# The sign of a 64-bit weight made by ScalarE's scaling, and the list scheduler's settings beside it

## The chip, the cores and the metric

One core of a Trainium2 chip runs the whole program in one launch. The metric is the device time of that launch in microseconds (us), the median of the runs shown. Engines: TensorE (PE, its weight loads PEld), VectorE (DVE), ScalarE (ACT), GpSimd (POOL) and SyncE (SP), which issues every DMA here.

## What is computed

Attention for 4 batches of 8 heads (576 tokens, head size 64), with every score more than tau below its row's maximum masked out, then two feed-forward networks over the 2304 tokens:

```python
scores = scale * np.matmul(q, k.transpose(0, 1, 3, 2))
thresh = np.max(scores, axis=-1, keepdims=True) - tau
scores = np.where(scores >= thresh, scores, -1000000000.0)
attn = softmax(scores)                       # written out in the reference
x = matmul(attn, v), heads side by side      # 2304 x 512
h = (x @ w1) * (x @ w2) @ w3
x = h @ w_out                                # 1024 -> 512
h = x @ w_in                                 # 512 -> 2048
out = (h * sigmoid(h)) @ w_out2              # 2048 -> 512
```

The weights arrive as 64-bit floats, all else as 32-bit.

## The kernel before

Nothing is in source order: each call describes one operation to a planner (`Plan.op`, with engine, estimated time, buffers read and written), and `Plan.run` then writes out a list schedule. It always takes the operation that can start first; a priority (`plan.base`) decides only among those that compete for an engine at that moment. `merge` gives the priorities: it interleaves a list of attention steps with a list of matrix-product steps by their cost and moves the attention steps forward by a lead (`LEAD` for the first merge, `LEADS[i]` for the next four).

The five merges are: attention of batch 0 beside the product w34 of w3 and w_out (`w34_step`, line 1181); then four times the layers of one token group (`moe_steps`, products on line 1131) beside the attention of the next batch, the last one alone. A group is 576, 432, 432 and 864 tokens, in tiles of 288 or 432.

A head pair's attention (`qtiles`): scores on line 759 into one of two PSUM slots, the row maximum by VectorE on line 726, then for each tile one of two ways to mask. Either ScalarE masks by a parametric ReLU (line 791) and exponentiates (line 799), or ScalarE exponentiates (line 809) and VectorE masks (line 817). `MASK_DVE` gives, for each batch, the share of the second way. For batches after 0 the result stays in the PSUM slot; for batch 0 it goes to SBUF tile e (`STAY`). Then high and low half of p (lines 858 and 865), transposes by DMA, and the product with v (line 935).

Precision is kept by splitting every 32-bit operand into a high part (ScalarE copy) and a low part (a subtraction, `pool_sub`, GpSimd on line 472, or VectorE on line 466 for every n-th one as `ON_DVE` says, keyed by kind and merge). Kind "w lo" splits weights, "split lo" splits activations.

The 64-bit weights are turned into 32-bit ones on the core, once: `load32` loads a tile in two DMAs, `words` converts it, and for group 0 the result is stored (line 1060) for the later groups to load. 36 tiles of 1 MB are converted, 12 of them (w3, w_out) in the first merge and 24 in the second. The conversion of one tile is a chain of four: ScalarE multiplies the high word, read as a 32-bit float, by 2 to the power -112 (line 1083); VectorE shifts the bits left by 3 (line 1090), puts the sign bit of the high word in (line 1097), and puts in the top of the low word (line 1105).

Of the kernel before, what the change touches and what calls it, by code (L numbers as in the profile page):

```python
# [7 lines left out]
F32 = mybir.dt.float32  # L8
F32R = mybir.dt.float32r
# [29 lines left out]
PSCALE = 2.0 ** 15  # L39
VSCALE = 2.0 ** 14  # L40

LEAD = 40.0
LEADS = 0.0, 40.0, 20.0, 0.0

EVERY = 100, 100

ON_DVE = {("w lo", 1): 3}

MASK_DVE = 0.4, 0.2, 0.6, 0.8

STAY = False, True, True, True
EARLY_OUT = False
KH_POOL = False

PORT = {"p lo", "w shift", "w sign", "w low", "w lo", "vl", "kl", "ql", "v scale"}
class Buf:


# [266 lines left out]
def fused_kernel(  # L325
# [21 lines left out]
    def pool(name, n, shape, dt):  # L347
        p = ctx.enter_context(tc.tile_pool(name=name, bufs=1))
        plan.cap(name, n)
        return buf(name, lambda slot: p.tile(shape, dt, tag=f"{name}{slot}", name=f"{name}{slot}"))  # L350

    def fixed(name, shape, dt):
        b = Buf()
        b.tile = const.tile(shape, dt, name=name)
        return b
# [21 lines left out]
    qk_b = pool("qk", 1, [128, 2, S], F32)  # L377
    vr_b = pool("vr", 1, [128, 2, 9, D], F32)
    vs_b = pool("vs", 2, [128, 16], F32)
    kh_b = pool("kh", 2, [128, S], F32R)  # L380
    kl_b = pool("kl", 2, [128, S], F32R)
    e_b = pool("e", 2, [128, S], F32)
    hl_b = pool("hl", 3, [128, 2 * S], F16)
    st_b = pool("st", 4, [128, 12], F32)
# [49 lines left out]
        return t.rearrange("p (a n) -> p a n", a=2)  # L434

    def mm(n, width, f32r=False):
        return n * max(width * 0.4167 + 2.5, 133.4 if f32r else 0.0) + 3

    def dma(kind, move, fn, r=(), w=(), hold=(), turn=False):
        plan.op(kind, "SP", plan.TURN_ISSUE if turn else plan.ISSUE, fn, r, w, hold, move, turn)  # L440
# [37 lines left out]
    sc = fixed("sc", [128, 1], F32)  # L478
    tau8 = fixed("tau8", [128, 1], F32)
    eb = fixed("eb", [128, 1], F32)  # L480
    qs = [[fixed(f"qs{j}{i}", [128, 640], F32R) for i in range(2)] for j in range(2)]
    vst = [fixed(f"vst{j}", [128, 14, 128], F16) for j in range(2)]
    ones = fixed("ones", [128, 128], F32)
    w34 = dram_p.tile([4, 128, 8, 128], F32, name="w34")
# [4 lines left out]
    def setup():  # L489
        dma("tau load", 56, lambda: nc.sync.dma_start(out=tau_sb.t, in_=tau), w=[tau_sb])  # L490

        def consts():


            nc.vector.tensor_scalar(
                out=tau8.t, in0=tau_sb.t, scalar1=0.0, scalar2=1.0, op0=ALU.is_ge, op1=ALU.subtract
            )
            nc.vector.tensor_scalar(
                out=sc.t, in0=tau8.t, scalar1=1.0, scalar2=0.125, op0=ALU.add, op1=ALU.mult
            )  # L500
            nc.vector.tensor_scalar(
                out=tau8.t, in0=tau8.t, scalar1=3.0e38, scalar2=None, op0=ALU.mult
            )
            nc.vector.scalar_tensor_tensor(
                out=tau8.t, in0=tau_sb.t, scalar=-8.0, in1=tau8.t, op0=ALU.mult, op1=ALU.min
            )
            nc.vector.tensor_tensor(out=eb.t, in0=sc.t, in1=tau8.t, op=ALU.mult)

        def zeros():
            for i in range(2):  # L510
                nc.vector.memset(qs[0][i].t[:, 576:640].bitcast(F32), 0.0)
                nc.vector.memset(qs[1][i].t[:, 0:64].bitcast(F32), 0.0)
            nc.vector.memset(ones.t, 1.0)

        plan.op("zeros", "DVE", 437, zeros, w=[*qs[0], *qs[1], ones])
        for j in range(2):
            plan.op(
                "v zeros", "POOL", 780,
                lambda j=j: nc.gpsimd.memset(vst[j].t[:, :, 64 - 64 * j:128 - 64 * j], 0.0),
                w=[vst[j]],  # L520
            )
        plan.op("consts", "DVE", 840, consts, r=[tau_sb], w=[sc, tau8, eb])
# [2 lines left out]
    raws, kst = {}, {}  # L525

    def load_qk(g):
        qk = qk_b()
        came = [Buf(), Buf()]
        if g:  # L530
            dma("qk load", 1638, lambda: nc.sync.dma_start(out=qk.t, in_=qkv[g, :, 0:2, :]), w=[qk])
            came = [qk, qk]
        else:
            for n in range(2):
                dma(
                    "qk load", 819,
                    lambda n=n: nc.sync.dma_start(out=qk.t[:, n], in_=qkv[g, :, n, :]),
                    w=[came[n]], hold=[qk],
                )
        raws[g] = (qk, came)  # L540

    def prep_qk(g):

        j, i = g % 2, (g // 2) % 2
        r, (cq, ck) = raws.pop(g)
        o = 0 if j == 0 else 64
        q = qs[j][i]
        kh, kl = kh_b(), kl_b()

        def sub(kind, out, a, b, need, w):  # L550
            if g:
                pool_sub(kind, S, out, a, b, need, w, [r])
            else:
                plan.op(
                    kind, "DVE", 676,
                    lambda: nc.vector.tensor_tensor(out=out(), in0=a(), in1=b(), op=ALU.subtract),
                    need, w, [r],
                )

        def copy(kind, out, a, need, w):  # L560
            if KH_POOL and 0 < g < 2 * NP:
                plan.op(kind, "POOL", 900, lambda: nc.gpsimd.tensor_copy(out=out(), in_=a()), need, w, [r])
            else:
                act_op(kind, S, lambda: nc.scalar.activation(out=out(), in_=a(), func=ACTF.Copy), need, w, [r])  # L564

        copy("qh", lambda: q.t[:, o:o + S], lambda: r.t[:, 0, :], [cq], [q])
        sub(
            "ql", lambda: q.t[64:128, o:o + S], lambda: r.t[64:128, 0, :],
            lambda: q.t[64:128, o:o + S].bitcast(F32), [cq, q], [q],
        )  # L570
        copy("kh", lambda: kh.t, lambda: r.t[:, 1, :], [ck], [kh])
        sub("kl", lambda: kl.t, lambda: r.t[:, 1, :], lambda: kh.t.bitcast(F32), [ck, kh], [kl])
        kst[g] = (kh, kl)

# [108 lines left out]
    def qtiles(pr, kinds):  # L683
# [3 lines left out]

        ga, gb = 2 * pr, 2 * pr + 1
        i = pr % 2
        qa, qb = qs[0][i], qs[1][i]  # L690
        n_t = len(kinds)
        st = st_b()
        k_s = [Buf() for _ in kinds]
# [60 lines left out]
            plan.base += 1e4  # L754

        def scores(sp, mms):
            for n, (q, o, k) in enumerate(mms):
                for a in range(2):
                    nc.tensor.matmul(  # L759
                        out=sp.t[:, a, 0:HALF], lhsT=q.t[:, o:o + 128],  # L760
                        rhs=k.t[:, a * HALF:(a + 1) * HALF],
                        start=(n == 0), stop=(n == len(mms) - 1),
                    )

        sps = []
        for n, (kind, c) in enumerate(kinds):
            if kind == "A":
                terms = [(qa, c * 128, kst[ga])]
            elif kind == "B":
                terms = [(qb, 128 + c * 128, kst[gb])]  # L770
            else:
                terms = [(qa, 512, kst[ga]), (qb, 0, kst[gb])]
            mms = [(q, o, k) for q, o, ks in terms for k in ks]
            sp = s_b()
            plan.op(
                "scores", "PE", len(mms) * mm(2, HALF, True), lambda sp=sp, mms=mms: scores(sp, mms),
                [q for q, _, _ in mms] + [k for _, _, k in mms], [sp],
            )
            sps.append(sp)
            thresholds(sp, n)  # L780
# [251 lines left out]
    def load32(src, key=None, keep=None, rs=None):  # L1032

        if src.dtype == F32:
            r = wr_b()  # L1040
            dma("w load", 1456, lambda: nc.sync.dma_start(out=r.t, in_=src), key, [r])
            return r
        r = rs[0] if rs else wr_b()
        d = r64_b()
        came = [Buf(), Buf()]
        for a in range(2):
            cut = slice(a * 512, (a + 1) * 512)
            dma(
                "w64 load", 1456,
                lambda cut=cut: nc.sync.dma_start(  # L1050
                    out=d.t[:, cut],
                    in_=src[:, cut].bitcast(I32).rearrange("p (n t) -> p n t", t=2),
                ),
                w=[came[a]], hold=[d],
            )
        n = 1024 // len(rs or [r])
        for i, r in enumerate(rs or [r]):
            words(d, r, came, i * n, n)
        if keep is not None:
            dma("w keep", 1456, lambda: nc.sync.dma_start(out=keep, in_=r.t), [r], key)  # L1060
        return r
# [4 lines left out]
    def words(d, r, came, c0, n):  # L1066
# [11 lines left out]
        def rf():  # L1078
            return f32(r.t)[:, 0:n]
# [1 line left out]
        act_op(  # L1081
            "w scale", n,
            lambda: nc.scalar.activation(
                out=rf(), in_=high().bitcast(F32), func=ACTF.Copy, scale=2.0 ** -112
            ),
            came, [r], hold=[d],
        )
# [3 lines left out]
                out=ri(), in0=ri(), scalar1=3, scalar2=None, op0=ALU.logical_shift_left  # L1091
            ),
            [r], [r],
        )
        plan.op(
            "w sign", "DVE", 73 + n * 1.042,
            lambda: nc.vector.scalar_tensor_tensor(
                out=ri(), in0=high(), scalar=-0x80000000, in1=ri(),
                op0=ALU.bitwise_and, op1=ALU.bitwise_or,
            ),  # L1100
            [r], [r], hold=[d],
        )
        plan.op(
            "w low", "DVE", 73 + n * 1.042,
# [396 lines left out]
```

## Time and profile before

| | us |
|---|---|
| median of 3 runs | 1023.28 |
| lowest, highest | 1021.57, 1027.87 |
| the profiled execution, time | 1024.79 |
| its span from first to last instruction | 1023.0 |
| busy in the span: PE, PEld | 960.1, 863.6 |
| busy in the span: DVE, ACT, POOL | 605.0, 684.6, 509.8 |

Some words on reading it. The span is one execution; busy time is what an engine spent in instructions that compute. Matmuls are pipelined and their ends are modelled, so that a PE that reads as busy need not run at its peak. An idle time before an instruction is put down to the releaser that came last. PEclk is the clock that TensorE was granted, as a share of the full one. The DMA share is the mean busy share of 16 DMA engines. In the views by line, a group shows the engine, the operation, what it writes and reads, the shapes, the count, then busy us and mean ns of one.

### The profile page before, as it was taken

To read this page: it belongs to the slowest core of one execution; us is meant where nothing else is said; L and a number is where in the kernel's file an instruction comes from. 1 tells how busy PE (TensorE), PEld (TensorE's weight loads), DVE (VectorE), ACT (ScalarE), POOL (GpSimd) and SP (SyncE) were. 2 spreads that over 40 slices of the span, in tenths; PEclk is the share of its full clock that TensorE was granted. 3 is DMA by queue.
4 is the path that set the end of the run, shared out by engine and by line. 5 is a ranking of instruction groups with operands and counts; after the bars stand their busy time and mean duration, and the time that the engine had idled before them with its cause. 6 is when DMAs were issued, how large, how long until landed. Compare 5 with 4: busy or idle time off the path is not lost.

```text
span 1023.0 us, 15583 instructions
## 1 busy us (share of the span) xinstructions
PE 960.1 (94%) x5488; PEld 863.6 (84%) x5488; DVE 605.0 (59%) x1238; ACT 684.6 (67%) x1225; POOL 509.8 (50%) x306
## 2 busy tenths in 40 slices
PE   3579998999899996999999999999999999999998
PEld 3455658999899886999999999889989999999998
DVE  6988988777888886667666766666721111210211
ACT  7868967887888977788988787788733322432430
POOL 2221132653564543576859666675744542652650
PEclk9879999999999998999999999999999999999999
DMA  7999999987799987677778886776641111111111
GB/s 227 210 241 232 264 259 284 266 231 209 195 255 271 244 224 198 153 183 190 186 193 186 210 204 184 161 181 153 154 127 62 62 50 54 62 62 42 62 59 53
DMA packets 213934, 175.09 MB, mean 171 GB/s; under 512 B 175328, under 2 KB 181472, under 8 KB 213856
## 3 DMA queue, kind: packets, MB, share of 16 engines
q1 hardware_dynamic: 213856, 174.10, 66.5%
q8 instruction: 43, 0.70, 0.3%
q14 instruction: 35, 0.29, 0.1%
HBM read 112.20 MB, written 19.40 MB: 129 GB/s over the span
## 4 chain that ended last, share of the span: by engine, by line
PE 68%; DMA 11%; DVE 8%; ACT 7%; issue 4%; POOL 2%; SPq 1%; ACTq 0%; DVEq 0%; POOLq 0%
PE banks L1131 55%; PE banks L759 6%; PE banks L935 5%; DMA qk<-qkv 3%; PE banks L1181 2%; DMA r<-w3t 2%; DVE hl L865 2%; DMA pt<-hl 1%; DMA r<-w 1%; DMA r<-win 1%; DVE banks L726 1%; DMA wr<-w 1%; ACT hl L858 1%; POOL lo L472 1%; ACT hi L453 1%
## 5 line engine op out<-in xcount | busy, mean ns | idle before, releaser
L1131 PE MATMUL banks<-acts,hi 128*128 128x432 f32 (+1 forms) x1664 | 417.7, 337 | 5.9 <-DVE tb L1317 4.9
L472 POOL TENSOR_TENSOR lo<-wr,hi 128x1024 fp32r<-128x1024 f32 x102 | 247.9, 2431 | 221.0 <-PE banks L1131 101.9
L1131 PEld LDWEIGHTS banks<-acts,hi 128*128 128x128 f32 x1664 | 290.8, 188 | 16.7 <-DVE tb L1317 6.9
L1131 PE MATMUL banks<-acts,lo 128*128 128x432 f32 (+1 forms) x832 | 278.0, 334 | 0.3 <-POOL lo L472 0.3
L1131 PE MATMUL banks<-x,hi 128*128 128x432 f32 (+1 forms) x1024 | 267.4, 345 | 2.2 <-POOL x L472 1.0
L472 POOL TENSOR_TENSOR acts<-tb,acts 128x432 fp32r<-128x432 f32 (+1 forms) x120 | 150.8, 1262 | 85.5 <-ACT acts L1218 84.9
L1131 PEld LDWEIGHTS banks<-x,hi 128*128 128x128 f32 x1024 | 184.2, 189 | 10.3 <-POOL x L472 1.3
L1131 PE MATMUL banks<-x,lo 128*128 128x432 f32 (+1 forms) x512 | 176.3, 344 | 0.1
L1131 PEld LDWEIGHTS banks<-acts,lo 128*128 128x128 f32 x832 | 156.2, 188 | 5.1 <-POOL lo L472 0.6
L453 ACT ACTIVATE hi<-wr 128x1024 fp32r<-128x1024 f32 x112 | 118.3, 1057 | 28.0 <-DMA wr<-w 15.2
L726 DVE TENSOR_REDUCE banks<-banks 128x1 f32<-128x576 f32 x144 | 106.8, 758 | 29.1 <-PE banks L759 28.6
L759 PE MATMUL banks<-kh,qs 128*128 128x288 f32 x320 | 82.0, 340 | 43.5 <-ACT e L799 16.4
L1317 DVE SCALAR_TENSOR_TENSOR tb<-ta,banks 128x432 f32<-128x432 f32 (+1 forms) x96 | 52.8, 550 | 108.0 <-ACT ta L1310 103.3
L935 PE MATMUL banks<-pt,vst 128*128 128x288 f16 x656 | 102.5, 297 | 5.9 <-DMA pt<-hl 5.6
L759 PEld LDWEIGHTS banks<-kh,qs 128*128 128x128 f32 x320 | 57.2, 204 | 57.7 <-ACT e L799 20.6
L472 POOL TENSOR_TENSOR qs<-qk,qs 64x576 fp32r<-64x576 f32 x31 | 49.1, 1585 | 111.5 <-ACT qs L564 89.2
L865 DVE SCALAR_TENSOR_TENSOR hl<-banks,st,hl 128x576 f16<-128x576 f32 x108 | 84.1, 812 | 31.3 <-ACT hl L858 30.7
L1131 PEld LDWEIGHTS banks<-x,lo 128*128 128x128 f32 x512 | 96.3, 188 | 3.4 <-POOL lo L472 0.3
L935 PEld LDWEIGHTS <-vst 128*128 128x128 f16 x656 | 60.1, 101 | 40.9 <-issue 20.2
L1218 ACT ACTIVATE acts<-tb 128x432 fp32r<-128x432 f32 (+1 forms) x120 | 70.5, 587 | 34.3 <-DVE tb L1317 22.3
L858 ACT ACTIVATE hl<-banks,st 128x576 f16<-128x576 f32 x108 | 75.1, 737 | 8.8 <-DVE st L831 8.6
L759 PE MATMUL banks<-kl,qs 128*128 128x288 f32 x320 | 73.3, 312 | 0.0
(82 smaller groups left out, 1126.7 us busy)
## 6 DMA issues: line engine op xcount, KB each, us to landing
wr<-w SPq DMA_DIRECT2D x88, 512.0 KB, 3.6
qk<-qkv SPq DMA_DIRECT2D x31, 576.0 KB, 4.8
r<-wo SPq DMA_DIRECT2D x24, 512.0 KB, 6.0
w<-wr SPq DMA_DIRECT2D x24, 512.0 KB, 3.5
vr<-qkv SPq DMA_DIRECT2D x16, 576.0 KB, 4.7
r<-w3t SPq DMA_DIRECT2D x16, 512.0 KB, 5.6
r<-w SPq DMA_DIRECT2D x16, 512.0 KB, 6.1
r<-win SPq DMA_DIRECT2D x16, 512.0 KB, 5.9
```

Source lines behind the costliest of these rows:

```text
L453: kind, n, lambda: nc.scalar.activation(out=out(), in_=a(), func=ACTF.Copy), r, w, hold, ns
L472: lambda: nc.gpsimd.tensor_tensor(out=out(), in0=a(), in1=b(), op=ALU.subtract),
L726: lambda: nc.vector.tensor_reduce(out=low(), in_=sp.t[:, :, 0:HALF], axis=AX.XY, op=ALU.max, negate=True),
L759: nc.tensor.matmul(out=sp.t[:, a, 0:HALF], lhsT=q.t[:, o:o + 128], rhs=k.t[:, a * HALF:(a + 1) * HALF], start=(n == 0), stop=(n == len(mms ...
L858: lambda: nc.scalar.activation(out=two(hl.t[:, 0:S]), in_=src(), func=ACTF.Copy, scale=r()),
L865: lambda: nc.vector.scalar_tensor_tensor(out=two(hl.t[:, S:2 * S]), in0=src(), scalar=r(), in1=two(hl.t[:, 0:S]), op0=ALU.mult, op1=ALU.su ...
L935: nc.tensor.matmul(out=ps[a].t[:, 0:HALF], lhsT=v2.t[:, n, :], rhs=pt.t[:, c, a * HALF:(a + 1) * HALF], start=(first and n == 0), stop=(fi ...
L1131: nc.tensor.matmul(out=ps.t[:, 0:n1 - n0], lhsT=a_.t[:, k * 128:(k + 1) * 128], rhs=x_.t[:, n0:n1], start=(n == 0 and i == 0), stop=(n == ...
L1181: lambda jb=jb, x=x: nc.tensor.matmul(out=ps.t[:, 0:512], lhsT=f32(r.t)[:, jb * 128:(jb + 1) * 128], rhs=x.t[:, 0:512].bitcast(F32), start ...
L1218: lambda: nc.scalar.activation(out=hi.t[:, at[0]:at[1]], in_=x32.t[:, 0:n], func=ACTF.Copy),
L1317: lambda ps=ps, t=t, n=n, o=o, g32=g32: nc.vector.scalar_tensor_tensor(out=g32.t[:, o:o + n], in0=t.t[:, 0:n], scalar=1.0, in1=ps.t[:, 0:n ...
```

## The change

ScalarE's scaling of the high word becomes a parametric ReLU with slope -(2 to the power 32) for negative inputs. For a negative weight the product is then positive with an exponent field larger by 32, and the shift left by 3 moves the bit of value 32 of that field into the sign's place. The VectorE operation for the sign, line 1097, is dropped.

With it settings change: the leads, the share of masks on VectorE, the subtractions on VectorE, and `EARLY_OUT`, by which batch 0's mask on ScalarE writes to SBUF tile e instead of back to the PSUM slot. The planner's price of a matmul of 32-bit floats is 0.4517 ns a column and 2.9 ns instead of 0.4167 and 2.5 with a floor of 133.4. Query and key of head 0 come by one DMA instead of two, and the four query tiles get their zeros a second time before their first use. The diff also holds a path for whole heads (`WHOLE`), which is 0, so that nothing of it is issued; buffers for q and k are named in another pool with the same sizes.

```diff
-LEAD = 40.0
-LEADS = 0.0, 40.0, 20.0, 0.0
+LEAD = 100
+LEADS = 20, 20, 40, 0

-ON_DVE = {("w lo", 1): 3}
-MASK_DVE = 0.4, 0.2, 0.6, 0.8
+ON_DVE = {("w lo", 1): 2, ("split lo", 1): 2}
+MASK_DVE = 0.5, 0.2, 0.6, 0.6

-EARLY_OUT = False
-KH_POOL = False
+EARLY_OUT = True
+WHOLE = 0
...
     def mm(n, width, f32r=False):
-        return n * max(width * 0.4167 + 2.5, 133.4 if f32r else 0.0) + 3
+        return n * (width * 0.4517 + 2.9 if f32r else width * 0.4167 + 2.5) + 3
...
-        came = [Buf(), Buf()]
-        if g:
-            dma("qk load", 1638, lambda: nc.sync.dma_start(out=qk.t, in_=qkv[g, :, 0:2, :]), w=[qk])
-            came = [qk, qk]
-        else:
-            for n in range(2):
-                dma(
-                    "qk load", 819,
-                    lambda n=n: nc.sync.dma_start(out=qk.t[:, n], in_=qkv[g, :, n, :]),
-                    w=[came[n]], hold=[qk],
-                )
-        raws[g] = (qk, came)
+        dma("qk load", 1638, lambda: nc.sync.dma_start(out=qk.t, in_=qkv[g, :, 0:2, :]), w=[qk])
+        raws[g] = (qk, [qk, qk])
...
+        if H * WHOLE <= g < H * WHOLE + 4:
+            plan.op("q zeros", "DVE", 70, lambda: q_zeros(j, i, False), w=[q])
...
             lambda: nc.scalar.activation(
-                out=rf(), in_=high().bitcast(F32), func=ACTF.Copy, scale=2.0 ** -112
+                out=rf(), in_=high().bitcast(F32), func=ACTF.Prelu, scale=2.0 ** -112,
+                alpha=-(2.0 ** 32),
             ),
...
-        plan.op(
-            "w sign", "DVE", 73 + n * 1.042,
-            lambda: nc.vector.scalar_tensor_tensor(
-                out=ri(), in0=high(), scalar=-0x80000000, in1=ri(),
-                op0=ALU.bitwise_and, op1=ALU.bitwise_or,
-            ),
-            [r], [r], hold=[d],
-        )
```

## Rows read from the trace of the kernel before

**Rows 1.** The page's slices, 40 of 25.6 us: busy tenths.

```profile
PE   3579998999899996999999999999999999999998
...
DMA  7999999987799987677778886776641111111111
```

**Rows 2.** Busy time by stretches; first row columns, first column length, last GB/s.

```profile
core 0: us, PE busy (x) PEld busy (x) DVE busy (x) ACT busy (x) POOL busy (x), PEclk, DMA share, GB/s
0.00:160.00 160.00, 124.23 (x532) 77.80 (x533) 135.03 (x291) 125.21 (x232) 35.76 (x27) 0.95 0.98 244
160.00:420.00 260.00, 240.68 (x1733) 229.16 (x1733) 209.06 (x368) 207.22 (x381) 126.59 (x68) 0.99 0.88 230
...
340.00:420.00 80.00, 67.38 (x447) 61.59 (x446) 59.65 (x115) 61.59 (x115) 36.95 (x21) 0.96 0.79 203
420.00:1023.00 603.00, 595.23 (x3227) 556.63 (x3224) 260.90 (x581) 352.14 (x615) 347.49 (x213) 1.00 0.49 127
```

**Rows 3.** Waits of PE, 0 to 160 us: waiter, releaser, us, times, longest.

```profile
PE banks L759 <- ACT e L799: 16.4, 8, 5.1
```

**Rows 4.** Waits of PE, 160 to 420 us.

```profile
PE banks L759 <- DVE hl L865: 11.9, 7, 5.5
```

**Rows 5.** Waits of SyncE's queue: two of 0 to 160, one of 160 to 420.

```profile
SPq L885 <- DVE hl L865: 22.4, 10, 4.2
SPq L885 <- DVE banks L726: 10.2, 4, 3.0
...
SPq L1060 <- DVE wr L1105: 21.7, 7, 6.2
```

**Rows 6.** Busy time of line 1097 (the sign) by stretches.

```profile
0.00:160.00 160.00, 17.62 (x18) 0.95 0.98 244
160.00:420.00 260.00, 29.19 (x22) 0.99 0.88 230
```

**Rows 7.** Line 1097 for whole tiles: shortest, median, longest in ns.

```profile
L1097 DVE SCALAR_TENSOR_TENSOR wr<-r,wr x24: 1197/1224/2450, 143.5 to 378.2; 128x1024 int32<-128x1024 int32 x24
```

**Rows 8.** ScalarE's groups by line and shape, whole span.

```profile
L858 ACT ACTIVATE hl<-banks,st 128x576 f16<-128x576 f32 x108 | 75.1, 737 | 8.8 <-DVE st L831 8.6
...
L791 ACT ACTIVATE banks<-banks,st 128x576 f32<-128x576 f32 x72 | 50.8, 709 | 14.9 <-DVE st L735 13.7 <-DVE vs L627 0.5 <-DVE st L831 0.5
...
L1083 ACT ACTIVATE wr<-r 128x1024 f32<-128x1024 f32 x24 | 27.5, 1144 | 11.2 <-DMA r<-w 6.3 <-DMA r<-wo 2.5 <-DMA r<-win 1.7
...
L564 ACT ACTIVATE qs<-qk 128x576 fp32r<-128x576 f32 x32 | 21.8, 683 | 9.2 <-DMA qk<-qkv 9.1
...
L799 ACT ACTIVATE e<-banks,eb,sc 128x576 f32<-128x576 f32 x22 | 18.2, 829 | 0.2
```

**Rows 9.** VectorE's groups by line and shape, whole span.

```profile
L466 DVE TENSOR_TENSOR lo<-wr,hi 128x1024 fp32r<-128x1024 f32 x10 | 14.6, 1462 | 1.4 <-ACT hi L453 1.1 <-PE banks L1131 0.3
...
L817 DVE SCALAR_TENSOR_TENSOR e<-banks,st,e 128x576 f32<-128x576 f32 x14 | 11.3, 808 | 4.4 <-ACT e L809 4.4
...
L556 DVE TENSOR_TENSOR kl<-qk,kh 128x576 fp32r<-128x576 f32 x1 | 0.8, 757 | 0.1
...
L511 DVE MEMSET qs<- 128x64 f32 x2 | 0.2, 112 | 0.8 <-PEq L1491 0.8
```

**Rows 10.** GpSimd's groups by line and shape, 160 to 420 us.

```profile
L472 POOL TENSOR_TENSOR lo<-wr,hi 128x1024 fp32r<-128x1024 f32 x21 | 53.1, 2529 | 52.7 <-ACT hi L453 22.3 <-PE banks L1131 14.1 <-ACT e L984 7.7
L472 POOL TENSOR_TENSOR acts<-tb,acts 128x576 fp32r<-128x576 f32 x24 | 42.7, 1778 | 37.3 <-ACT acts L1218 37.2
...
L472 POOL TENSOR_TENSOR x<-e,x 128x576 fp32r<-128x576 f32 x4 | 5.7, 1423 | 16.9 <-ACT x L1006 16.8
```

**Rows 11.** Busy time of line 1181 on PE, 60 to 100 us.

```profile
60.00:100.00 40.00, 21.30 (x46) 0.88 1.00 241
```

**Rows 12.** DMA issues of q and k: count, KB each, us to landing.

```profile
qk<-qkv SPq DMA_DIRECT2D x31, 576.0 KB, 4.8
...
qk<-qkv SPq DMA_DIRECT2D x2, 288.0 KB, 3.3
```

More of the change, by code (lines that the diff above doesn't have):

```diff
@@ L40 @@
 VSCALE = 2.0 ** 14
-LEAD = 40.0
-LEADS = 0.0, 40.0, 20.0, 0.0
+LEAD = 100
+LEADS = 20, 20, 40, 0
 EVERY = 100, 100
-ON_DVE = {("w lo", 1): 3}
-MASK_DVE = 0.4, 0.2, 0.6, 0.8
+ON_DVE = {("w lo", 1): 2, ("split lo", 1): 2}
+MASK_DVE = 0.5, 0.2, 0.6, 0.6
 STAY = False, True, True, True
-EARLY_OUT = False
-KH_POOL = False
-PORT = {"p lo", "w shift", "w sign", "w low", "w lo", "vl", "kl", "ql", "v scale"}
+EARLY_OUT = True
+WHOLE = 0
+PORT = {"p lo", "w shift", "w low", "w lo", "vl", "kl", "ql", "v scale"}
 class Buf:
@@ L379, in fused_kernel @@
     vs_b = pool("vs", 2, [128, 16], F32)
-    kh_b = pool("kh", 2, [128, S], F32R)
-    kl_b = pool("kl", 2, [128, S], F32R)
+    kh_b = own("kh", 2, [128, S], F32R)
+    kl_b = own("kl", 2, [128, S], F32R)
+    k_b = [
+        buf(n, lambda slot, n=n: mem.tile([128, S], F32, tag=f"{n}{slot}", name=f"{n}w{slot}"))
+        for n in ("kh", "kl")
+    ]
     e_b = pool("e", 2, [128, S], F32)
@@ L480, in fused_kernel, with q_tile, q_zeros @@
     eb = fixed("eb", [128, 1], F32)
-    qs = [[fixed(f"qs{j}{i}", [128, 640], F32R) for i in range(2)] for j in range(2)]
+    qs = [[Buf() for _ in range(2)] for _ in range(2)]
+    def q_tile(j, i, whole):
+        dt = F32 if whole else F32R
+        return once(f"qs{j}{i}", f"q{'w' if whole else 's'}{j}{i}", [128, 640], dt)
+    def q_zeros(j, i, whole):
+        o = 576 if j == 0 else 0
+        a = q_tile(j, i, whole)[:, o:o + 64]
+        nc.vector.memset(a if whole else a.bitcast(F32), 0.0)
     vst = [fixed(f"vst{j}", [128, 14, 128], F16) for j in range(2)]
@@ L510, in zeros @@
             for i in range(2):
-                nc.vector.memset(qs[0][i].t[:, 576:640].bitcast(F32), 0.0)
-                nc.vector.memset(qs[1][i].t[:, 0:64].bitcast(F32), 0.0)
+                q_zeros(0, i, WHOLE > 0)
+                q_zeros(1, i, WHOLE > 0)
             nc.vector.memset(ones.t, 1.0)
@@ L527, in load_qk @@
     def load_qk(g):
-        qk = qk_b()
-        came = [Buf(), Buf()]
-        if g:
-            dma("qk load", 1638, lambda: nc.sync.dma_start(out=qk.t, in_=qkv[g, :, 0:2, :]), w=[qk])
-            came = [qk, qk]
-        else:
-            for n in range(2):
-                dma(
-                    "qk load", 819,
-                    lambda n=n: nc.sync.dma_start(out=qk.t[:, n], in_=qkv[g, :, n, :]),
-                    w=[came[n]], hold=[qk],
-                )
-        raws[g] = (qk, came)
+        if g < H * WHOLE:
+            j, i = g % 2, g // 2 % 2
+            k, o = k_b[j](), 0 if j == 0 else 64
+            dma(
+                "q load", 450,
+                lambda: nc.sync.dma_start(
+                    out=q_tile(j, i, True)[0:64, o:o + S], in_=qkv[g, 0:64, 0, :]
+                ),
+                w=[qs[j][i]],
+            )
+            dma(
+                "k load", 450,
+                lambda: nc.sync.dma_start(out=k.t[0:64], in_=qkv[g, 0:64, 1, :]), w=[k],
+            )
+            kst[g] = (k,)
+            return
+        qk = qk_b()
+        dma("qk load", 1638, lambda: nc.sync.dma_start(out=qk.t, in_=qkv[g, :, 0:2, :]), w=[qk])
+        raws[g] = (qk, [qk, qk])
     def prep_qk(g):
+        if g < H * WHOLE:
+            return
         j, i = g % 2, (g // 2) % 2
@@ L548, in prep_qk, with qt @@
         kh, kl = kh_b(), kl_b()
+        if H * WHOLE <= g < H * WHOLE + 4:
+            plan.op("q zeros", "DVE", 70, lambda: q_zeros(j, i, False), w=[q])
+        def qt():
+            return q_tile(j, i, False)
         def sub(kind, out, a, b, need, w):
-            if g:
+            if g or WHOLE:
                 pool_sub(kind, S, out, a, b, need, w, [r])
@@ L560, in copy @@
         def copy(kind, out, a, need, w):
[L561 to L566, printed above, removed]
-        sub(
-            "ql", lambda: q.t[64:128, o:o + S], lambda: r.t[64:128, 0, :],
-            lambda: q.t[64:128, o:o + S].bitcast(F32), [cq, q], [q],
+            act_op(kind, S, lambda: nc.scalar.activation(out=out(), in_=a(), func=ACTF.Copy), need, w, [r])
+        copy("qh", lambda: qt()[:, o:o + S], lambda: r.t[:, 0, :], [cq], [q])
+        sub(
+            "ql", lambda: qt()[64:128, o:o + S], lambda: r.t[64:128, 0, :],
+            lambda: qt()[64:128, o:o + S].bitcast(F32), [cq, q], [q],
         )
@@ L689, in qtiles @@
         i = pr % 2
-        qa, qb = qs[0][i], qs[1][i]
+        whole = ga < H * WHOLE
+        rows = slice(0, 64 if whole else 128)
         n_t = len(kinds)
@@ L756, in scores @@
         def scores(sp, mms):
-            for n, (q, o, k) in enumerate(mms):
+            for n, (j, o, k) in enumerate(mms):
                 for a in range(2):
                     nc.tensor.matmul(
-                        out=sp.t[:, a, 0:HALF], lhsT=q.t[:, o:o + 128],
-                        rhs=k.t[:, a * HALF:(a + 1) * HALF],
+                        out=sp.t[:, a, 0:HALF], lhsT=q_tile(j, i, whole)[rows, o:o + 128],
+                        rhs=k.t[rows, a * HALF:(a + 1) * HALF],
                         start=(n == 0), stop=(n == len(mms) - 1),
@@ L767, in qtiles @@
             if kind == "A":
-                terms = [(qa, c * 128, kst[ga])]
+                terms = [(0, c * 128, kst[ga])]
             elif kind == "B":
-                terms = [(qb, 128 + c * 128, kst[gb])]
+                terms = [(1, 128 + c * 128, kst[gb])]
             else:
-                terms = [(qa, 512, kst[ga]), (qb, 0, kst[gb])]
-            mms = [(q, o, k) for q, o, ks in terms for k in ks]
+                terms = [(0, 512, kst[ga]), (1, 0, kst[gb])]
+            mms = [(j, o, k) for j, o, ks in terms for k in ks]
             sp = s_b()
             plan.op(
-                "scores", "PE", len(mms) * mm(2, HALF, True), lambda sp=sp, mms=mms: scores(sp, mms),
-                [q for q, _, _ in mms] + [k for _, _, k in mms], [sp],
+                "scores", "PE", len(mms) * (mm(2, 4 * HALF) if whole else mm(2, HALF, True)),
+                lambda sp=sp, mms=mms: scores(sp, mms),
+                [qs[j][i] for j, _, _ in mms] + [k for _, _, k in mms], [sp],
             )
```

## The prediction

> **What bounds the kernel now.** I read the page's slices first. They show TensorE thin for the first three slices and nearly full from the fourth, and the DMA engines at seven to nine tenths until slice 15, with a dip around slices 10 and 11 [rows 1]. The table by stretches says the same in microseconds [rows 2]. In the first 160 us (attention of batch 0 and the product of w3 and w_out) TensorE is busy for 124.2 us, so it idles 35.8; in 160 to 420 us (the first layers of group 0 beside attention of batch 1) it idles 260 - 240.7 = 19.3, and 12.6 of these lie in the last 80 us of that stretch. After 420 us it idles 603 - 595.2 = 7.8 us, about four of them the tail behind the last product. So whatever this change can give lies before 420 us: 55.1 us of idle array, no more, apart from what a faster clock in the first slices adds (0.95 granted in the first stretch).
>
> Next I looked at what ends that idle time. In the first 160 us the largest entry is the scores' matmuls (line 759) waiting for the exponential of an earlier tile (line 799): 16.4 us in 8 waits [rows 3]. The two PSUM slots for scores are held until that exponential is through. In the second stretch it is the same line waiting for VectorE's low half of p (line 865), 11.9 us in 7 waits [rows 4]. The DMA queue of SyncE, though its engines look full, itself stands still for VectorE: 22.4 and 10.2 us in the first stretch for transposes whose input is not there, and 21.7 us in the second before the store of a converted weight (line 1060) [rows 5]. VectorE and ScalarE together are busy 135.0 + 125.2 = 260.2 us of 160, then 209.1 + 207.2 = 416.3 us of 260 [rows 2]. I read the front as a chain that goes to and fro between these two engines, with transfers not far behind.
>
> **The sign.** Line 1097 goes: 17.6 us of VectorE in the first stretch and 29.2 in the second [rows 6]. In its place ScalarE's line 1083 becomes a parametric ReLU with the same count of elements. Its price is bounded by ScalarE's rows at 576 columns: the existing parametric ReLU of line 791 takes 709 ns, a plain copy 683 (line 564), a copy with a scale read from memory 737 [rows 8]. That is from 26 to 54 ns more for each of the 40 conversions, 1.0 to 2.2 us in all; nothing is excluded below, since the first of these reads PSUM and the second SBUF, but a gain has no reason. I take 1.2 us, spread over 345 us, and so next to nothing. The Trainium skill ("ScalarE: Activation LUTs", What ACT_TABLE_LOAD costs) says each pointer operand adds about 93 ns, which by an estimate from that page would make 3.7 us for a bias pointer; the rows here show a third to a half of it. The conversion chain of one weight (copy, shift, sign, low word) loses one link of 1.22 us at its median [rows 7], so its buffer is free that much sooner and the store behind it in SyncE's queue is issued that much sooner; 7 waits of line 1060 lose at most 8.5 us of queue time.
>
> **What is added to VectorE.** MASK_DVE for batch 0 rises from 0.4 to 0.5: 14 of 36 masks become 18, four more at 808 ns and some 0.2 us of small operations, 4.1 us, while ScalarE sheds four times 709 ns = 2.8 us [rows 8, 9]. Four extra memsets of 64 columns cost 4 x 112 ns = 0.45 us [rows 9]. In the second stretch every second instead of every third low half of a weight goes to VectorE, five or so more at 1462 ns = 7.3 us, and half of the 24 split low halves of 576 columns at the 757 ns of line 556's row = 9.1 us [rows 9]; GpSimd is relieved of 5 x 2.53 + 12 x 1.78 = 34 us of its 126.6 [rows 2, 10]. Net for VectorE: -17.6 + 4.1 + 0.45 = -13.1 us in the first stretch, -29.2 + 7.3 + 9.1 = -12.8 us in the second. For batch 3 MASK_DVE falls from 0.8 to 0.6: seven masks back to ScalarE, where TensorE is full beside them [rows 2]; without that cover seven times 709 ns, 5 us, would show.
>
> **From engine time to span.** First stretch: both engines' 260.2 us fall by 13.1 + 2.8 - 0.5 = 15.4, or 5.9%; if the stretch follows their sum it loses 9.5 us. Nothing, if transfers set its pace (DMA share 0.98) [rows 2]; 13.1, if VectorE alone does. I take 8, nearer the sum, because SyncE's queue waits for VectorE and not the other way about [rows 5]. Second stretch: 416.3 falls by 12.8 - 0.7 = 12.1 or 2.9%, 7.6 us by the same rule, at most the 19.3 us of idle array, at least nothing. I take 6; the chain split low half to next product also gets shorter by 1.78 - 0.76 = 1 us in half of the cases.
>
> **EARLY_OUT** lets the mask of batch 0 write to SBUF and the exponential work there, so a score slot is free one exponential earlier, 829 ns [rows 8]. Eight waits of [rows 3] by 0.83 are 6.6 us at most; nothing, if the next tile then waits for VectorE's maximum. Many of these waits are several microseconds long and end behind a queue of other work, so I take 2.
>
> **First load.** Query and key of the first head come in one transfer instead of two: 4.8 us from issue to landing instead of 3.3 [rows 12]. The first scores come 0.5 to 1.5 us later; nothing hides it, I take +0.7.
>
> **Priorities.** LEAD 100 exceeds the 37.6 + 55.2 = 92.8 cost units of the first merge, so every operation of attention of batch 0 outranks every one of the w3 times w_out product. The planner still starts whatever can start first; rank decides between operations that compete. Attention may end sooner and the products may end later. LEADS 20 instead of 0 pulls attention of batch 1 forward, towards the 12.6 us of idle array at 340 to 420 us [rows 2]. I set both at nothing in the sum, with bounds of -6 (half of those 12.6) and +14 (the rival below). The matmul prices in the planner and the last two LEADS change the order after 420 us, where 7.8 us of idle can be had or doubled; nothing, -3 to +4.
>
> **Sum.** -8 - 6 - 2 + 0.7 = -15.3 us. On the profiled execution's 1024.8 us (span 1023.0) that is 1009.5; the median of the runs is 1023.3, so 1008.
>
> **Rivals.** (a) *Transfers set the pace.* The DMA share is 0.98 over the first 160 us and 0.88 over the next 260, and no byte is saved. For it: the digits 9 of the first eight slices [rows 1]. Against: the queue waits for VectorE [rows 5]. Then only the second stretch's last 80 us, at a share of 0.79, gain their part, 80/260 x 7.6 = 2.3, and two or three from the queue's shorter waits, less 0.7: 1019.
>
> (b) *VectorE and GpSimd keep each other out.* The sign's row has a median of 1224 ns and a longest of 2450 [rows 7], and GpSimd's split subtraction takes 1778 ns where the same width and operation elsewhere in the stretch takes 1423 [rows 10]; both stretch while the other engine works. The 17 subtractions that move to VectorE could each wait out a whole GpSimd subtraction of 2.53 us at worst, 43 us, or half of one on average, 21 us; that turns -12.8 into +8 for VectorE, and the second stretch gains nothing: 1023.3 - 9.3 = 1014. Against it: the sign itself is such an operation, and 22 of them leave that stretch. The Trainium skill ("SBUF — State Buffer", SBUF: two separate sides) calls this an exclusive lock for a whole instruction, against a VectorE operation with two SBUF inputs, and by that rule the moved subtractions are of the kind that block. The longest row agrees with it.
>
> (c) *Slower: the lead starves the array.* By 100 us 21.3 us of w3 times w_out are done [rows 11], in gaps of attention. If attention, now ahead in every contest for ScalarE, VectorE and the queue, does not end sooner, that work moves behind it, into a stretch with 19.3 us of scattered idle that can take back perhaps a third; 14 us are lost, and with no other gain left in a front that waits for the array, the time is about 1037. It decides when fewer than about half of these 46 matmuls come before 100 us while the first product of line 1131 still starts at 160 us.
>
> **How the numbers follow.** Forecast 0.50 (its own range 995 to 1013), (a) 0.28, (b) 0.08, (c) 0.14. A measurement of this kernel tells about 1% from no change, that is 1013 to 1033.5. From the forecast nearly all, 0.48, and 0.02 from (b) fall below: 0.50 faster; slower holds (c) but for 0.01, the part of it below 1033.5: 0.13; the rest 0.37 is the same. The range takes in the forecast and (a) to its upper side, and leaves 0.04 below and 0.14 above: 996 to 1027.
>
> **What would show it.** Right: the first product of line 1131 starts before 155 us; VectorE's busy time before 420 us is some 26 us smaller; the waits of line 759 for line 799 in the first stretch fall under 10 us. Line 1083 should read 1.15 to 1.20 us. Wrong: the DMA share rises to 1 in the first stretch with its length unchanged (a); line 466 well above 1.5 us (b); line 1181 beginning after 90 us with line 1131 no earlier than now (c); or idle array after 420 us above 12 us, from the new order alone.

## The result and the profile after

| | before | after |
|---|---|---|
| median, us | 1024.72 (4 runs) | 1010.87 (4 runs) |
| ratio, with its 95% interval | | 0.9866 [0.9839, 0.9893] |
| profiled execution, us | 1024.79 | 1010.97 |
| its span, us | 1023.0 | 1009.2 |

The kernel is 1.3% faster, 13.9 us by the medians. The forecast was 1008 with a range of 996 to 1027, so time and direction came as told. The experiments below show that the way to them was wrong, and the agreement luck: the sum put nearly all of the gain on the sign and nothing on the leads, and neither of the two gives anything alone.

Line numbers move in the changed kernel: scores 759 to 787, mask 791 to 820, exponential 799 to 828, VectorE's mask 817 to 846, low half of p 865 to 894, weight scaling 1083 to 1113, low word 1105 to 1128, products 1131 to 1154, w34 1181 to 1204, store 1060 to 1090, GpSimd's subtraction 472 to 478, VectorE's 466 to 472. In the kernel before with the sign operation taken out, the lines behind it move up by seven: products 1131 to 1124, low word 1105 to 1098.

Busy time of the changed kernel by stretches, with the columns of [rows 2]; its span ends at 1009.2 us:

```profile
0.00:160.00 160.00, 131.78 (x591) 85.17 (x592) 126.10 (x303) 130.11 (x238) 33.80 (x27) 0.96 0.99 252
160.00:420.00 260.00, 246.89 (x1780) 236.34 (x1779) 196.13 (x379) 214.48 (x396) 102.03 (x58) 1.00 0.89 238
340.00:420.00 80.00, 77.63 (x523) 73.64 (x522) 59.69 (x120) 63.96 (x118) 37.10 (x22) 1.00 0.79 197
420.00:1009.20 589.20, 578.15 (x3121) 538.80 (x3119) 241.38 (x527) 343.18 (x600) 332.84 (x205) 1.00 0.48 124
```

Against [rows 2] the array idles 28.2 us in the first 160 us instead of 35.8, and 2.4 instead of 12.6 at 340 to 420 us. VectorE is busy 322.2 us before 420 us instead of 344.1, 21.9 less where some 26 had been foretold. After 420 us the array idles 11.0 us instead of 7.8.

The waits of the array in the first 160 us of the changed kernel (waiter, releaser, us, times, longest), the three largest:

```profile
PE banks L787 <- DVE e L846: 15.2, 8, 3.0
PE banks L787 <- DVE qs L586: 6.7, 1, 6.7
PE banks L787 <- ACT e L820: 4.6, 6, 1.6
```

The wait for the exponential, 16.4 us in [rows 3], is gone. In its place stand waits for ScalarE's mask, 4.6 us, and for VectorE's mask, which the kernel before had too, but only at 8.7 us:

```profile
PE banks L759 <- DVE e L817: 8.7, 3, 4.5
```

In the changed kernel's rows the second is the start: the first scores wait 6.7 us for head 0, with query and key in one transfer. In the kernel before they began at 5.9 us.

Two landmarks cut the span at the work itself and not at the clock: the first product of the layers, and the first product of 432 columns, with which group 1 begins. (It is the first of four steps, one for each head pair; the last of the four needs the last pair of batch 1.) For the changed kernel, the first from the view of line 1154 (shortest, median, longest ns, then first and last start), the second from the timeline:

```profile
L1154 PE MATMUL banks<-x,hi x1024: 289/357/697, 152.6 to 967.9; 128*128 128x432 f32 x128, 128*128 128x288 f32 x43
```

```profile
389.55 0.56 PE L1154 MATMUL banks<-x,hi 128*128 128x432 f32 x2
```

The same two in the kernel before:

```profile
L1131 PE MATMUL banks<-x,hi x1024: 289/356/562, 160.4 to 981.1; 128*128 128x432 f32 x128, 128*128 128x288 f32 x43
```

```profile
399.53 0.56 PE L1131 MATMUL banks<-x,hi 128*128 128x432 f32 x2
```

By these landmarks the first part falls from 160.4 to 152.6 us, the second from 239.1 to 237.0, and the rest of the span from 623.5 to 619.6: 7.8, 2.1 and 3.9 us.

### The profile page after: what moved, and what is told of

Same layout as the page of the kernel before. It is cut to its first block, busy times and chain, and to the rows that moved or that the text cites. A ratio compares the mean times of both kernels' runs of the same rounds, so it can differ in the third digit from the quotient of the medians.

```text
span 1009.2 us, 15550 instructions
## 1 busy us (share of the span) xinstructions
PE 956.8 (95%) x5488; PEld 860.3 (85%) x5488; DVE 563.6 (56%) x1207; ACT 687.8 (68%) x1233; POOL 468.7 (46%) x289
## 4 chain that ended last, share of the span: by engine, by line
PE 61%; DMA 10%; ACT 10%; DVE 9%; issue 7%; POOL 2%; SPq 0%; ACTq 0%; POOLq 0%; DVEq 0%
PE banks L1154 49%; PE banks L964 4%; PE banks L787 4%; PE banks L1204 3%; DMA pt<-hl 2%; DVE banks L754 2%; DVE hl L894 2%; DMA qk<-qkv 2%; DMA wr<-w 2%; DMA vr<-qkv 2%; ACT hl L887 1%; POOL lo L478 1%; DMA r<-wo 1%; ACT banks L828 1%; ACT hi L459 1%
## 5 line engine op out<-in xcount | busy, mean ns | idle before, releaser
L478 POOL TENSOR_TENSOR lo<-wr,hi 128x1024 fp32r<-128x1024 f32 x97 | 234.0, 2413 | 259.9 <-PE banks L1154 144.1
L459 ACT ACTIVATE hi<-wr 128x1024 fp32r<-128x1024 f32 x112 | 118.7, 1061 | 59.3 <-PE banks L1154 28.2
L478 POOL TENSOR_TENSOR acts<-tb,acts 128x432 fp32r<-128x432 f32 (+1 forms) x108 | 126.0, 1172 | 62.8 <-ACT acts L1241 61.8
L787 PE MATMUL banks<-kh,qs 128*128 128x288 f32 x320 | 79.8, 333 | 30.6 <-DVE e L846 15.2
L478 POOL TENSOR_TENSOR qs<-qk,qs 64x576 fp32r<-64x576 f32 x31 | 45.5, 1468 | 115.0 <-ACT qs L591 94.0
```

The costliest lines, as they stand in the source:

```text
L459: kind, n, lambda: nc.scalar.activation(out=out(), in_=a(), func=ACTF.Copy), r, w, hold, ns
L478: lambda: nc.gpsimd.tensor_tensor(out=out(), in0=a(), in1=b(), op=ALU.subtract),
L787: nc.tensor.matmul(out=sp.t[:, a, 0:HALF], lhsT=q_tile(j, i, whole)[rows, o:o + 128], rhs=k.t[rows, a * HALF:(a + 1) * HALF], start=(n == ...
```

## The experiments

Ratios are to the kernel before, with 95% intervals. In the order in which they ran; the first four, the next four and the last four were measured together.

**The sign alone.** The kernel before, with

```diff
-                func=ACTF.Copy, scale=2.0 ** -112
+                func=ACTF.Prelu, scale=2.0 ** -112, alpha=-(2.0 ** 32),
-        plan.op("w sign", "DVE", ...)
```

> The kernel before with the parametric ReLU in place of the sign operation and no other edit. Theory A (VectorE's time in the front carries the gain): 46.8 us leave VectorE before 420 us; with VectorE and ScalarE sharing the front (260 of 160 us and 416 of 260 us busy) the span falls by 0.5 x 17.6 x 160/135 or so in the first stretch and 6 in the second, 10 to 16 us in all: 1008 to 1014. Theory B (the settings carry it, the front is paced by transfers): 0 to 4 us, 1020 to 1024. Theory C (the planner's reshuffling moves the time at random): anything within the size that the placebo shows.

Measured: 1031.8 us, 1.0069 [1.0051, 1.0087]. It is slower, though 46.8 us of VectorE are gone and nothing is added. Theory A falls in this form, and B's range is missed on the far side. The first product starts at 155.6 us, 4.8 earlier than before, but group 1 begins at 404.4 us, 4.9 later. What the array waits for around the start of group 1 (385 to 430 us), sign alone:

```profile
PE banks L759 <- DVE hl L865: 3.9, 1, 3.9
PE banks L1124 <- DVE e L992: 2.5, 1, 2.5
```

Line 992 is the output of attention of batch 1: the first product of group 1 waits for the end of that attention. Line 865 is a low half of p, but of batch 2: this wait ends at 409.7 us, when batch 1's last product with v (399.2 us) is long over. In the order written out for PE, batch 2's scores, which need a slot that batch 2's own first tiles still hold, stand among the first products of group 1. When attention of batch 1 ends can be read directly: its output is 16 operations of line 992, two for each head, and the last of them starts at 401.3 us in the kernel before and at 406.9 with the sign alone:

```profile
L992 DVE SCALAR_TENSOR_TENSOR e<-banks,vs,e x16: 502/517/525, 216.7 to 401.3; 64x288 f32<-64x288 f32 x16
```

```profile
L992 DVE SCALAR_TENSOR_TENSOR e<-banks,vs,e x16: 501/517/524, 191.2 to 406.9; 64x288 f32<-64x288 f32 x16
```

Busy time at 400 to 420 us, sign alone and then the kernel before, columns of [rows 2]:

```profile
400.00:420.00 20.00, 13.57 (x65) 12.41 (x65) 14.18 (x32) 14.23 (x27) 4.55 (x3) 0.74 0.72 172
```

```profile
400.00:420.00 20.00, 14.13 (x68) 12.90 (x67) 12.52 (x30) 13.59 (x27) 8.30 (x6) 0.83 0.67 142
```

With the sign alone the array idles 6.4 of these 20 us and the granted clock, mean 0.74, drops to the lower of its two levels for part of them. The clock had been 1.00 in the 20 us before. The kernel before has the same stop, 5.9 us idle and a clock of 0.83; the changed kernel has none, it is busy for all 20 us at 1.00. So the stop is not what makes the sign alone slower than the kernel before, but what both have and the changed kernel has not.

**The settings alone.** The changed kernel with the copy and VectorE's sign operation put back.

```diff
-                func=ACTF.Prelu, scale=2.0 ** -112, alpha=-(2.0 ** 32),
+                func=ACTF.Copy, scale=2.0 ** -112
+        plan.op("w sign", "DVE", ...)
```

> The changed kernel with the plain copy and VectorE's sign operation put back; leads, masks, subtractions, early score release, prices and first load stay as changed. Theory A: VectorE then has more work than in the kernel before (+4.5 us in the first stretch, +16 in the second), so no gain and perhaps a loss: 1020 to 1032. Theory B: most of the gain, 1010 to 1015.

Measured: 1054.69 us, 1.0298 [1.0277, 1.0319]. Beyond theory A's range, and B falls. With these settings the sign's 46.8 us on VectorE cost 1054.69 - 1010.87 = 43.8 us, nearly one for one.

**The sign twice.** The kernel before with a second copy of the operation, which puts in a bit that is already there.

```diff
+        plan.op("w sign", "DVE", ...)   # once more
```

> The kernel before with the sign operation issued twice in a row (the second puts in the bit that is already there): 46.8 us more on VectorE before 420 us. Theory A: 8 to 18 us slower, the mirror of the sign alone: 1031 to 1041. Theory B: within 4 us of the kernel before.

Measured: 1073.78 us, 1.0476 [1.0444, 1.0507]: 49.8 us for 46.8 us of added VectorE time, far more than the 8 to 18 that theory A said. VectorE is busy 144.0 of the first 160 us:

```profile
0.00:160.00 160.00, 119.11 (x500) 74.39 (x501) 144.02 (x304) 122.10 (x226) 31.36 (x25) 0.94 0.92 225
```

So here VectorE's time is worth about its length when it is added, and nothing when it is taken away alone.

**A placebo for the order.** The kernel before, with one estimate of the planner moved by 2 ns; the instructions are the same, their order is not.

```diff
-                "max", "DVE", 680,
+                "max", "DVE", 682,
```

> The kernel before with the planner's estimate for the row maximum 682 ns instead of 680; no instruction is added, removed or altered, only the written-out order can differ. Theories A and B: within 3 us of the kernel before, 1020 to 1026. Theory C (random reshuffling decides): it differs by 5 us or more either way, and then no difference of that size between other runs can be put down to its edit.

Measured: 1025.74 us, 1.0022 [1.0004, 1.0041], within 3 us. A new order by itself moves the whole by about 0.2%, but the parts by more: the first product starts at 158.7 us and group 1 at 407.1, so the second part takes 248.4 us and not 239.1, and the rest gives 3.7 us back. It is one sample. The second part of the kernel before seems a short one among kernels with a lead of 0 there: the sign alone took 248.8. The sign alone, 0.7% slower, lies outside this one sample's 0.2%. A difference of two or three us between two of these kernels is not put down to its edit here.

**Four settings put back, one at a time, in the changed kernel.**

```diff
-EARLY_OUT = True
+EARLY_OUT = False
```

> The changed kernel with the early release of the score slots off. Theory V (VectorE's load decides the front, the settings only place the freed time): the slots of batch 0 are held 0.83 us longer in up to 18 tiles, 2 to 6 us slower than the changed kernel, 1013 to 1017. Theory O (the written-out order decides, and each setting fits the others): 8 us or more slower, 1019 and above, with more waiting of SyncE's queue at line 1090's store than the 34.7 us of the changed kernel.

```diff
-LEAD = 100
+LEAD = 40.0
```

> The changed kernel with the first merge's lead back at 40. Theory V: no engine gets more work, within 4 us of the changed kernel, 1007 to 1015. Theory O: 8 us or more slower, 1019 and above; the first product of the layers then starts later than 152.6 us.

```diff
-LEADS = 20, 20, 40, 0
+LEADS = 0.0, 40.0, 20.0, 0.0
```

> The changed kernel with the leads of the four later merges back at 0, 40, 20, 0. Theory V: within 4 us of the changed kernel, 1007 to 1015. Theory O: 8 us or more slower, with idle array again at 340 to 420 us (12.6 us in the kernel before, 2.4 in the changed one).

```diff
-ON_DVE = {("w lo", 1): 2, ("split lo", 1): 2}
+ON_DVE = {("w lo", 1): 3}
```

> The changed kernel with the subtractions of the second merge back as they were: VectorE loses 17 of them (about 19 us), GpSimd gains them (about 34 us, at 127 of 260). Theory V: less VectorE, same or faster, 1003 to 1011. Theory O: 8 us or more slower, 1019 and above. A third, Theory G (GpSimd's slow subtractions delay products and the conversion's buffers): 3 to 8 us slower, with the array waiting for line 478 in the second stretch.

| put back | us | ratio | minus the changed kernel, % |
|---|---|---|---|
| EARLY_OUT | 1012.53 | 0.9896 [0.9881, 0.9911] | +0.3 |
| LEAD | 1010.5 | 0.9880 [0.9860, 0.9900] | +0.1 |
| LEADS | 1028.72 | 1.0064 [1.0039, 1.0089] | +2.0 |
| ON_DVE | 1014.09 | 0.9911 [0.9894, 0.9928] | +0.5 |

Three of the four hardly matter, nearly as theory V has it (ON_DVE is a little on the slow side and out of V's range, where theory G puts it, but without waits of the array for line 478), and the fourth takes away the whole gain, as theory O has it. Neither theory was right for all. The early release of the score slots does what the edit says and yet brings next to nothing: with it off the array waits 13.0 us for the exponential in the first stretch and only 2.6 for VectorE's mask, with it on none for the exponential and 15.2 us for that mask.

**The pair.** The kernel before, with the sign and the four leads, and nothing else.

```diff
-LEADS = 0.0, 40.0, 20.0, 0.0
+LEADS = 20, 20, 40, 0
-                func=ACTF.Copy, scale=2.0 ** -112
+                func=ACTF.Prelu, scale=2.0 ** -112, alpha=-(2.0 ** 32),
-        plan.op("w sign", "DVE", ...)
```

> The kernel before with two edits only: the parametric ReLU for the sign, and the leads of the four later merges 20, 20, 40, 0. Theory P (these two are the pair that carries the change; neither does alone): within 4 us of the changed kernel, 1007 to 1015. Rival Q (the gain needs the whole set of settings): about half way or less, 1018 to 1030.

Measured: 1000.72 us, 0.9783 [0.9764, 0.9803]. The pair carries the whole gain and more, beyond theory P's range on the fast side, and rival Q falls: this version beats the kernel before by 2.2% and the changed kernel by 0.8%. Its landmarks:

```profile
L1124 PE MATMUL banks<-x,hi x1024: 289/357/467, 147.9 to 957.1; 128*128 128x432 f32 x128, 128*128 128x288 f32 x43
```

```profile
384.46 0.55 PE L1124 MATMUL banks<-x,hi 128*128 128x432 f32 x2
```

And attention of batch 1 ends 20 us earlier than in the kernel before:

```profile
L992 DVE SCALAR_TENSOR_TENSOR e<-banks,vs,e x16: 499/516/524, 176.6 to 380.9; 64x288 f32<-64x288 f32 x16
```

**The leads alone.** The kernel before with `LEADS = 20, 20, 40, 0`.

> The kernel before with the leads 20, 20, 40, 0 and nothing else; VectorE's sign operation stays. Theory P: the leads alone give nothing as long as VectorE carries the sign, 1020 to 1030. Rival R (the leads alone carry the gain, and the sign is worth nothing): 1008 to 1015. If it is well above 1035, the leads are what made the settings without the sign slow; if it is below 1030, VectorE's added subtractions and masks are.

Measured: 1029.13 us, 1.0059 [1.0038, 1.0081]. Rival R falls, and the leads are not what made the settings alone slow: they cost 6 of some 31 us. The subtractions and masks that those settings add to VectorE are left as the likely cause of the rest, but they were not tried by themselves with the sign on VectorE. The last sign operation of a whole tile starts at 391.4 us, in the kernel before at 378.2 [rows 7]:

```profile
L1097 DVE SCALAR_TENSOR_TENSOR wr<-r,wr x24: 1196/1221/2457, 141.3 to 391.4; 128x1024 int32<-128x1024 int32 x24
```

and in 160 to 412 us the products wait for VectorE's multiplication (line 1317), where the kernel before had 4.9 us in 5 waits:

```profile
PE banks L1131 <- DVE tb L1317: 10.4, 10, 3.3
```

Attention of batch 1 ends late too, in spite of the lead, and group 1 begins at 412.7 us:

```profile
L992 DVE SCALAR_TENSOR_TENSOR e<-banks,vs,e x16: 500/516/524, 179.7 to 408.6; 64x288 f32<-64x288 f32 x16
```

**The first of the four leads put back**, in the changed kernel.

```diff
-LEADS = 20, 20, 40, 0
+LEADS = 0, 20, 40, 0
```

> The changed kernel with only the lead of the second merge back at 0 (0, 20, 40, 0). Theory P in its narrow form (the attention of batch 1, late beside group 0, holds up group 1): as slow as all four leads put back, 1023 to 1032, with the first product of 432 columns at 395 us or later (389.6 in the changed kernel). Rival: the later leads carry it, within 4 us of the changed kernel.

Measured: 1027.1 us, 1.0053 [1.0036, 1.0070], as slow as with all four put back. So it is the lead of attention of batch 1 over group 0. The last output of that attention starts at 399.3 us instead of 384.4, group 1 begins at 399.7 us, and the wait of the sign-alone kernel at 385 to 430 us is back:

```profile
PE banks L787 <- DVE hl L894: 4.9, 1, 4.9
PE banks L964 <- DMA pt<-hl: 2.8, 2, 2.2
```

**That lead at 40.**

```diff
-LEADS = 20, 20, 40, 0
+LEADS = 40, 20, 40, 0
```

> The changed kernel with the lead of the second merge at 40 instead of 20. Theory P: the attention of batch 1 is no longer the last thing at 20, so more lead gives nothing, 1008 to 1016. Rival: the lead was still too small, 4 us or more faster, below 1007, and the first product of 432 columns before 386 us.

Measured: 1013.96 us, 0.9910 [0.9887, 0.9933]. More lead gives nothing: the last output of attention of batch 1 starts 10 us earlier, at 374.8 us instead of 384.4, and group 1 begins no sooner, at 392.3 us. With a lead of 20 attention is no longer what comes last.

## Why the prediction was right in its number and wrong in its working

The four kernels of sign and leads, all else as before:

| | leads 0, 40, 20, 0 | leads 20, 20, 40, 0 |
|---|---|---|
| sign by VectorE | 1 | 1.0059 [1.0038, 1.0081] |
| sign by ScalarE | 1.0069 [1.0051, 1.0087] | 0.9783 [0.9764, 0.9803] |

Each edit alone loses a little, the two together gain 2.2%; the part that belongs to neither is 0.9783 / (1.0059 x 1.0069) = 0.966, some 35 us. Nor does it look like the chance of one written-out order: with the sign gone from VectorE, six kernels with a first lead of 20 or 40 take 1000.7 to 1014.1 us and three with 0 take 1027.1 to 1031.8. The step that failed is "From engine time to span": it turned a smaller sum of busy time into a shorter span in proportion, 8 and 6 us, without asking what would come last once that time was gone. And "Priorities" set the leads at nothing, with -6 as the best case: putting the first of them back costs 16.2 us.

What the rows show in their place is two streams that both must be through before group 1 can run. One is the layers of group 0, for which VectorE converts weights; the other is attention of batch 1, which shares that engine. Four kernels and the first lead put back, by the last start of a conversion's low word, the last output of attention of batch 1, and the first product of group 1:

| us | last low word | last output of attention | group 1 begins |
|---|---|---|---|
| kernel before | 380.8 | 401.3 | 399.5 |
| sign alone | 373.7 | 406.9 | 404.4 |
| leads alone | 392.9 | 408.6 | 412.7 |
| the pair | 364.1 | 380.9 | 384.5 |
| the changed kernel | 362.4 | 384.4 | 389.6 |
| first lead put back in it | 372.9 | 399.3 | 399.7 |

The sign's removal alone ends the conversions sooner and attention later; the lead alone leaves both late, since VectorE still carries the sign; the two together end both some 17 to 20 us sooner. In every kernel with a first lead of 0 the array also stops, right after group 1's first products, in front of batch 2's scores (line 759 or 787 waiting for line 865 or 894): 5.5 us before, 3.9 with the sign alone, 3.3 in the placebo, 3.1 with the sign twice (at 447 us), 5.1 and 4.9 with all leads or the first put back. In every kernel measured with that lead at 20 or 40 and the sign gone from VectorE (the changed one, with EARLY_OUT, LEAD or ON_DVE put back, the pair, lead 40) no such wait stands there, and none either with the leads alone, where the waits lie before group 1. This stop lies behind the landmark, so that putting the first lead back costs 11.2 us in the second part and 8.2 behind it.

That pattern is shown by the landmarks and waits; why the second part shortens by just as much as it does was not taken apart, since products, conversions and buffers pace each other there. By the landmarks of the profiled executions 29.3 of 38.1 us that belong to neither edit alone lie in the second part, and 20.0 if the placebo stands for the kernel before.

Point by point:

- *The front bounded by VectorE and ScalarE to and fro.* Right for added work: the sign twice cost 49.8 us for 46.8. Wrong as a price for removed work.
- *First stretch -9.3 with early release and first load.* The first part shortened by 7.8 us. The sign alone gave 4.8 of these, the pair 12.5, with the same settings of the first merge; the 7.7 us between them are not explained. The leads alone gave 3.9 and the placebo 1.7, so a new order moves this part too.
- *EARLY_OUT -2.* Right in size: putting it back costs 1.7 us by the medians, intervals overlapping. The lower bound is near what happened, though not for the reason given: the next wait is for VectorE's mask, not for its maximum.
- *Second stretch -6, and LEADS nothing.* The two terms should have been one. By landmarks that part shortened by only 2.1 us against the kernel before, but in the placebo, the same instructions in another order, it takes 9 us more than those 239.1 us.
- *After 420 us nothing, -3 to +4.* From group 1's first product on the span fell 3.9 us, with 3.3 us more idle array after 420 us; the test of "above 12 us" was not met, at 11.0.
- *The parametric ReLU +26 to 54 ns.* No price at all; see below. Beside the 93 ns that are cited there these rows are 0.28 to 0.58 of it, a little wider than "a third to a half".
- *The store issued sooner.* Its waits in SyncE's queue for the low word did not shrink by up to 8.5 us; at 160 to 420 us they grew from 21.7 us [rows 5] to 34.7, in 9 waits (line 1090).
- *First load +0.7.* The first scores start at 6.66 instead of 5.95 us, 0.7 later, as said.
- *Rival (a), transfers.* The share is 0.99 in the first 160 us, as before, and the first part is shorter, with 252 GB/s moved instead of 244, so the share of 0.98 did not bound the pace before.
- *Rival (b), the engines keeping each other out.* VectorE's subtractions of weights take 1362 ns on average where 1.5 us was the mark, and GpSimd's of 576 columns got faster, 1529 instead of 1778 ns. With ON_DVE put back the kernel is 0.5% slower, not faster, so (b) falls as a cause that decides. Single meetings are there (1597 ns against a median of 756, at 355.1 us, while a GpSimd subtraction runs until 356.0):

```profile
L472 DVE TENSOR_TENSOR acts<-tb,acts x12: 747/756/1597, 172.9 to 365.5; 128x576 fp32r<-128x576 f32 x12
```

  With them the mean of this row is 944 ns, not the 757 that the sum took, and all 27 moved or kept subtractions together are 4.4 us above their medians.

- *Rival (c), the lead starving the array.* It does not: w34 begins at 65.5 us instead of 70.6, and 21.0 us of it are done at 60 to 100 us, as in [rows 11]; LEAD 40 or 100 makes no difference.
- *The signs of being right.* The earlier first product (152.6 us) and the lost wait for the exponential came, VectorE's drop came short (21.9 of some 26 us), and line 1113 reads 1.144 us, under the 1.15 to 1.20 named. None of them could tell the sum's working from that of the pair.

What stays open: the changed kernel is 0.8% slower than the pair. By landmarks 4.7 us of the 10.2 lie before the first product, 0.4 in the second part (237.0 and 236.6 us), and 5.1 after it. The edits that differ are LEAD, MASK_DVE, ON_DVE, EARLY_OUT, the planner's prices, the first load and the extra zeros. LEAD, ON_DVE and EARLY_OUT, put back singly, gain at most 0.4 us, so one of the others, or some of these together, or the written-out order costs it. In the first stretch the scores wait 15.2 us for VectorE's mask against 8.9 in the pair and 6.7 us at the start against 5.7, but the pair has 8.0 us of waits for the exponential, which the changed kernel has not. Masks, prices and first load were not tried by themselves.

## What to carry to other kernels

Busy time taken from a loaded engine was worth something here only where that engine's work is what ends last; ask which other stream meets it at the next join, and whether that stream's priority was set for the old load. Price an edit and the priorities beside it as one term, and measure both alone and together: a two by two table cost three kernels here and overturned a sum that had come out right. And where a list scheduler writes the order, run a placebo first, so that it is known how much a new order moves by itself (0.2% of the whole here, 9 us in a part, by one sample).

## What was not expected of the hardware

The parametric ReLU costs ScalarE nothing over a copy: line 1113 against [rows 8].

```profile
L1113 ACT ACTIVATE wr<-r 128x1024 f32<-128x1024 f32 x24 | 27.5, 1144 | 9.0 <-DMA r<-w 3.2 <-DVE lo L472 2.0 <-DMA r<-wo 1.9
```

Both means are 1144 ns. The forecast took 26 to 54 ns more, from rows of other shapes and sources. The Trainium skill ("ScalarE: Activation LUTs", What ACT_TABLE_LOAD costs) gives the same time per element for every function, which agrees, and about 93 ns for each pointer operand; if the bias of the parametric ReLU is such an operand here, which the row does not show, the measured difference of 0 ns stands against it.
